# Streaming v twice: 256 instead of 128 columns in each product of the attention sums

## The chip, the cores and the metric

The kernel runs on one core of a Trainium2 chip. The metric is the device time of one execution in microseconds, lower is better. A core has TensorE (PE; its weight loads are listed as PEld), VectorE (DVE), ScalarE (ACT), GpSimd (POOL), SyncE (SP) and 16 DMA engines.

## The reference

A sampled attention is followed by a feed-forward block that only 128 tokens of each batch pass through. Sizes are B = 8 batches, H = 8 heads, S = 576 positions, head size 64, 32 memory slots, D = 512, F = 1024, capacity 128.

```python
a = exp(phi - max(phi)) ; a = a / (sum(a) + 1e-9)     # over the 32 slots
k_m = einsum('bhsm,bhsd->bhmd', a, k)
v_m = einsum('bhsm,bhsd->bhmd', a, v)                 # the sums that the change touches
attn = softmax(q @ k_m.T / sqrt(64))
x = (attn @ v_m)                                      # heads joined: (B, S, 512)
scores = einsum('bsd,d->bs', x, w_gate)
for b in range(B):
    top_idx = argpartition(-scores[b], 128)[:128]
    ye = maximum(x[b, top_idx] @ w1, 0) @ w2
    out[b, top_idx] = x + sigmoid(scores) * ye        # other rows: out = x
```

## The kernel before

The softmax of phi is written out in some thirty VectorE and ScalarE instructions per batch (two chains take the batches in turn). `keys` turns its result over on TensorE (line 559), writes it to DRAM in two parts (`aparts`) and forms k_m (line 598). `split_v` writes v to DRAM in two parts as well (`vparts`).

The sums v_m are formed in `values`. The positions of a batch are cut into 48 chunks of T = 12 steps. Four batches are live at a time, one in each band of 32 partitions, and one accumulator bank of PSUM (`accs`) belongs to each. Batches 0 to 3 begin 6 chunks apart, batches 4 to 7 follow 48 chunks later in the same bands, which makes 114 chunks. For a chunk, `a_loader` (SyncE, line 640) fetches the softmax rows into `a_flat`, `widener` (lines 688 and 690, on VectorE or ScalarE) spreads them into `a_rows` (two buffers), and `v_loader` (POOL's queue, line 664) fetches `v_rows` (three buffers). A buffer is filled again when the products of the chunk that read it are through. Then each step issues one product for each live batch (line 709): the stationary operand is 32 rows by 128 columns of `a_rows`, the moving operand 32 rows by 128 values of `v_rows`, both in fp32r, and the result is added in 128 columns of the batch's bank.

When a batch's sums are complete, line 725 turns them over, `centre`, `scores` and `attend` (lines 770 to 933) do the attention, `rank` (lines 944 to 993) chooses the 128 tokens, and `forward` (lines 1055 to 1104) gathers them and runs two layers in fp32 (lines 1075 and 1093).

All of these are generators. `in_order_of_time` picks the next one by times that `Plan` keeps while the program is written: it books a duration for every instruction and, for TensorE, an amount of activity, from which `speed` decides which of the two clocks it books next. For products in fp32r the duration is `share`, set by `values` from the number of live batches, and the activity goes with the columns of `rhs`. While it books the lower clock, `forward` is given preference. So each engine's order is fixed when the program is written; on the chip each engine runs its own queue in that order.

Of the kernel before, what the change touches and what calls it, by code (L numbers as in the profile page):

```python
# [21 lines left out]
P = 128  # L22
# [164 lines left out]
def kernel(  # L187
# [15 lines left out]
    nc = Machine(plan, tc.nc)  # L203
# [6 lines left out]
    NG = phiT.shape[1]  # L210
    H = NG * NPR
    Dh = D // H
# [3 lines left out]
    SET = 4  # L216
# [5 lines left out]
    def first(b):  # L222
        return b // SET * STEP + b % SET * LAG
# [18 lines left out]
    accs = [psum.tile([P, 512], F32, name=f"acc{i}") for i in range(SET)]  # L242
# [28 lines left out]
    def take(n=1):  # L271
        while len(banks) < n:
            yield lambda: len(banks) >= n
        got = [first_free() for _ in range(n)]
        return got if n > 1 else got[0]
# [84 lines left out]
    def copy(dst, src):  # L360
        nc.scalar.activation(dst, src, AF.Copy)
        return plan.end
# [252 lines left out]
    def live(ch):  # L615
        return [b for b in range(B) if first(b) <= ch < first(b) + n_pieces]
# [82 lines left out]
    def values():  # L699
        for ch in range(COLS // T):  # L700
            while ch >= len(widened) or ch >= len(v_loaded):
                yield lambda: ch < len(widened) and ch < len(v_loaded)
            yield max(widened[ch], v_loaded[ch])
            vr, ar = v_rows[ch % NV], a_rows[ch % NB]
            plan.share = 256.0 / len(live(ch))
            for s in range(T):
                for b in live(ch):
                    p = slice(b % SET * 32, b % SET * 32 + 32)
                    nc.tensor.matmul(out=accs[b % SET][:, :P].rearrange("p (g d) -> p g d", d=Dh),  # L709
                                     lhsT=ar[p, s].rearrange("p j m -> p (j m)"), rhs=vr[p, :, s],  # L710
                                     start=(ch == first(b) and s == 0),
                                     stop=(ch == first(b) + n_pieces - 1 and s == T - 1))
                if s % 3 == 2 and s < T - 1:
                    yield plan.free["pe"]
            used_up.append(plan.end)
            b = live(ch)[0]
            if ch == first(b) + n_pieces - 1:
                yield
                turned = work.tile([P, P], F32, name="turned", tag="vz", bufs=1)
                copy(turned, accs[b % SET][:, :P])  # L720
                if b >= B - SET:
                    banks.append([plan.end, accs[b % SET]])
                yield
                bk = yield from take()
                nc.tensor.transpose(out=bk([P, P]), in_=turned, identity=ident)
                yield
                copy(v_m[b], bk([P, P]))
                bk.give()
                summed[b] = plan.end
# [382 lines left out]
    def load_weights():  # L1112
# [26 lines left out]
        (0.5 * 1e3, keys()), (0.0 * 1e3, split_v()),  # L1139
        (0.0, phi_loader()), (0.0, k_loader()), (0.0, q_loader()), (0.0, a_loader()), (0.0, v_loader()), (0.0, widener()),  # L1140
        (0.0 * 1e3, values()), (0.0 * 1e3, attentions(0)), (0.0 * 1e3, attentions(1)),
        (None and None * 1e3, forward(B * nt)), (0.0, load_weights())])

# [48 lines left out]
```

## Time and profile before

| what | value |
|---|---|
| median of three runs | 799.24 us |
| profiled execution, its own time | 798.46 us |
| its span, first to last instruction | 796.8 us |
| PE busy | 567.5 us, 71% |
| DVE busy | 587.7 us, 74% |
| ACT busy | 364.8 us, 46% |
| POOL busy | 235.6 us, 30% |
| products of the sums (line 709) | 4608, 265.7 us busy |

The span lies inside the execution's own time; 1.7 us lie around it. Busy time counts a time in which at least one instruction of the engine runs; products overlap on TensorE, so a mean duration is longer than the spacing of products. The clock column (PEclk) is the share of 2.4 GHz that was granted.

### The profile page before, as it was taken

To read this page: it belongs to the slowest core of one execution; us is meant where nothing else is said; L and a number is where in the kernel's file an instruction comes from. 1 tells how busy PE (TensorE), PEld (TensorE's weight loads), DVE (VectorE), ACT (ScalarE), POOL (GpSimd) and SP (SyncE) were. 2 spreads that over 40 slices of the span, in tenths; PEclk is the share of its full clock that TensorE was granted. 3 is DMA by queue.
4 is the path that set the end of the run, shared out by engine and by line. 5 is a ranking of instruction groups with operands and counts; after the bars stand their busy time and mean duration, and the time that the engine had idled before them with its cause. 6 is when DMAs were issued, how large, how long until landed. Compare 5 with 4: busy or idle time off the path is not lost. (4 is left out here: it accounts for less than half of the span.)

```text
span 796.8 us, 17830 instructions
## 1 busy us (share of the span) xinstructions
PE 567.5 (71%) x6898; PEld 462.8 (58%) x6898; DVE 587.7 (74%) x1043; ACT 364.8 (46%) x649; POOL 235.6 (30%) x419
## 2 busy tenths in 40 slices
PE   0002046145282499688997999999998999999994
PEld 0001045045271488677876778868877768766672
DVE  5999999999999999689628565658524387687700
ACT  3344462456355476464625436355634246434310
POOL 5022343423322233324314122315344142211200
PEclk9999999999999999999998558669899679899998
DMA  6046755879746577889666454548665434311110
GB/s 176 0 158 206 249 184 198 297 205 274 235 156 200 153 239 247 259 240 278 192 211 209 140 163 135 186 127 269 200 204 173 141 111 128 121 66 47 60 40 18
DMA packets 70348, 137.32 MB, mean 172 GB/s; under 512 B 14064, under 2 KB 46832, under 8 KB 70256
## 3 DMA queue, kind: packets, MB, share of 16 engines
q0 software_dynamic: 21824, 79.72, 30.4%
q1 hardware_dynamic: 48432, 56.39, 24.5%
q8 instruction: 56, 0.92, 0.5%
q14 instruction: 36, 0.29, 0.1%
HBM read 96.21 MB, written 39.85 MB: 171 GB/s over the span
## 5 line engine op out<-in xcount | busy, mean ns | idle before, releaser
L709 PE MATMUL acc<-v_rows,a_rows 32*128 32x128 f32 x4608 | 265.7, 360 | 60.1 <-ACT a_rows L690 32.4
L709 PEld LDWEIGHTS acc<-v_rows,a_rows 32*128 32x128 f32 x4608 | 245.2, 270 | 105.9 <-issue 43.4
L664 POOL DMA_DIRECT2D v_rows<-vparts x228 | 130.6, 580 | 284.5 <-PE acc L709 283.3
L690 ACT ACTIVATE a_rows<-a_flat,block_of 128x384 fp32r<-128x384 f32 x264 | 143.1, 604 | 137.1 <-PE acc L709 61.5
L688 DVE TENSOR_SCALAR a_rows<-a_flat,block_of 128x384 fp32r<-128x384 f32 x192 | 71.8, 419 | 80.1 <-PE acc L709 37.9
L559 PE MATMUL bank<-ident,ph 128*96 128x128 f32 x96 | 26.6, 432 | 77.3 <-DVE ph L464 77.3
L559 PEld LDWEIGHTS bank<-ident,ph 128*96 128x96 f32 x96 | 16.5, 198 | 81.4 <-issue 63.2
L598 PE MATMUL bank<-kb,aS 96*32 96x64 f32 x768 | 25.5, 308 | 51.6 <-DMA kb<-in_k 51.6
L1075 PE MATMUL bank<-xeT,w 128*128 128x128 f32 x416 | 57.0, 294 | 1.4 <-ACT xeT L1059 1.4
L1075 PEld LDWEIGHTS bank<-xeT,w 128*128 128x128 f32 x416 | 52.7, 205 | 4.1 <-ACT xeT L1059 1.8
L1093 PE MATMUL bank<-w,hT 128*128 128x512 f32 x96 | 54.8, 703 | 0.0
L533 POOL DMA_DIRECT2D vparts<-vlo x32 | 18.2, 569 | 121.5 <-DVE vlo L529 115.0
L598 PEld LDWEIGHTS bank<-kb,aS 96*32 96x32 f32 x768 | 19.9, 164 | 56.0 <-issue 26.1
L874 PE MATMUL bank<-vbd,eT 128*128 128x256 f32 x120 | 47.9, 546 | 0.0
L965 DVE SCALAR_TENSOR_TENSOR marks<-row,tg,wide 128x576 bf16<-128x576 f32 x40 | 32.7, 818 | 10.7 <-ACT row L949 9.0
L918 POOL DMA_DIRECT2D out<-xj x24 | 16.4, 682 | 64.7 <-DVE xj L914 55.4
L874 PEld LDWEIGHTS bank<-vbd,eT 128*128 128x128 f32 x120 | 29.7, 269 | 7.4 <-issue 1.7
L961 ACT ACTIVATE marks<-row,tg 128x576 bf16<-128x576 f32 x40 | 31.0, 775 | 1.8
L1093 PEld LDWEIGHTS bank<-w,hT 128*128 128x128 f32 x96 | 19.7, 222 | 17.7 <-issue 15.5
L461 DVE SCALAR_TENSOR_TENSOR ph<-rh,sm,ph 128x576 f32<-128x576 f16 x32 | 25.9, 810 | 4.3 <-ACT rh L450 4.3
L905 DVE TENSOR_TENSOR xj<-bank,rd 128x512 f32<-128x512 f32 x30 | 20.2, 684 | 10.8 <-PE bank L874 9.3
L924 DVE TENSOR_TENSOR prod<-xj,wg 128x512 f32<-128x512 f32 x40 | 27.4, 684 | 0.4
(163 smaller groups left out, 940.9 us busy)
## 6 DMA issues: line engine op xcount, KB each, us to landing
v_rows<-vparts POOLq DMA_DIRECT2D x156, 192.0 KB, 4.2
a_flat<-aparts SPq DMA_DIRECT2D x312, 48.0 KB
vb<-in_v SPq DMA_DIRECT2D x32, 288.0 KB
kb<-in_k SPq DMA_DIRECT2D x32, 288.0 KB
vparts<-vlo POOLq DMA_DIRECT2D x32, 288.0 KB, 2.9
vparts<-vb POOLq DMA_DIRECT2D x32, 288.0 KB, 4.0
qb<-in_qT SPq DMA_DIRECT2D x16, 576.0 KB
out<-xj POOLq DMA_DIRECT2D x16, 512.0 KB, 3.2
```

The costliest lines, as they stand in the source:

```text
L559: nc.tensor.transpose(out=bk([PT, 3, P])[:, c], in_=a[:, c0 + c], identity=ident)
L598: nc.tensor.matmul(out=km[j * M:(j + 1) * M], lhsT=aS[g][:, j, c], rhs=kb[:, j, c % (NC // 2)], start=(c == 0), stop=(c == NC - 1))
L664: nc.gpsimd.dma_start(out=v_rows[ch % NV].bitcast(F32)[32 * r0 + g:32 * r1:2, g] .rearrange("p s d -> p (s d)"), in_=src[:, ch * T * Dh:(c ...
L688: nc.vector.tensor_scalar_mul(ar[:, :, j], src, block_of[:, j:j + 1])
L690: nc.scalar.activation(ar[:, :, j], src, AF.Copy, scale=block_of[:, j:j + 1])
L709: nc.tensor.matmul(out=accs[b % SET][:, :P].rearrange("p (g d) -> p g d", d=Dh), lhsT=ar[p, s].rearrange("p j m -> p (j m)"), rhs=vr[p, :, s],
L874: nc.tensor.matmul(out=o([P, D])[:, g * 4 * Dh:(g + 1) * 4 * Dh], lhsT=eT[:, g, c * P:(c + 1) * P], rhs=vbd[b % 2][:, g].rearrange("p j d ...
L924: nc.vector.tensor_mul(prod, x[:, c], wg)
L961: nc.scalar.activation(sign, row, AF.Sign, bias=g, scale=-1.0, accum_out=less[:, c:c + 1])
L965: nc.vector.scalar_tensor_tensor(out=cmp, in0=row, scalar=g, in1=wide[:, off:off + S], op0=ALU.is_equal, op1=ALU.mult, accum_out=equal[:, ...
L1075: nc.tensor.matmul(out=bk([P, 4, P])[:, f, :n], lhsT=w1_sb[d][:, (f0 + f) * P:(f0 + f + 1) * P], rhs=xeT[:, d, :n], start=(d == 0), stop=( ...
L1093: nc.tensor.matmul(out=ps[:n], lhsT=hT[:, f, :n], rhs=w2_sb[f], start=(f == 0), stop=(f == KF - 1))
```

## The change

Each product of the sums takes the 128 values of v twice, by a repeat with stride 0 in the access pattern of the moving operand, and adds its result in 256 columns of the accumulator bank. The second 128 columns hold the same sums as the first; lines 720 and after read the first 128 alone. The bank has 512 columns. The number of products, their stationary operands and all transfers stay the same. `Plan.matmul` counts the cells of `rhs`, so the activity it books for these products doubles; the duration that it books stays.

```diff
             for s in range(T):
                 for b in live(ch):
                     p = slice(b % SET * 32, b % SET * 32 + 32)
-                    nc.tensor.matmul(out=accs[b % SET][:, :P].rearrange("p (g d) -> p g d", d=Dh),
-                                     lhsT=ar[p, s].rearrange("p j m -> p (j m)"), rhs=vr[p, :, s],
+                    nc.tensor.matmul(out=accs[b % SET][:, :2 * P].rearrange("p (r g d) -> p r g d", g=NG, d=Dh),
+                                     lhsT=ar[p, s].rearrange("p j m -> p (j m)"),
+                                     rhs=vr[p, :, s].unsqueeze(1).to_broadcast([32, 2, NG, Dh]),
                                      start=(ch == first(b) and s == 0),
                                      stop=(ch == first(b) + n_pieces - 1 and s == T - 1))
                 if s % 3 == 2 and s < T - 1:
```

## Rows read from the trace of the kernel before

**Rows 1.** The page's slices: 40 equal parts of the span, busy tenths.

```profile
PE   0002046145282499688997999999998999999994
DVE  5999999999999999689628565658524387687700
```

**Rows 2.** Windows of all engines: busy us (instructions), granted clock, DMA share, GB/s.

```profile
core 0: us, PE busy (x) PEld busy (x) DVE busy (x) ACT busy (x) POOL busy (x), PEclk, DMA share, GB/s
263.70:289.70 26.00, 19.56 (x372) 18.28 (x376) 25.93 (x35) 15.21 (x19) 10.13 (x16) 1.00 0.67 208
289.70:385.00 95.30, 79.67 (x1390) 72.32 (x1386) 81.01 (x124) 56.56 (x94) 32.39 (x56) 1.00 0.82 246
385.00:417.70 32.70, 32.35 (x363) 25.92 (x359) 12.78 (x35) 12.55 (x30) 8.34 (x15) 1.00 0.68 206
417.70:701.10 283.40, 273.03 (x3422) 218.49 (x3421) 170.11 (x428) 132.20 (x291) 89.68 (x156) 0.78 0.52 162
500.00:600.00 100.00, 99.32 (x1554) 79.50 (x1553) 54.76 (x136) 47.97 (x99) 37.20 (x64) 0.83 0.63 196
```

**Rows 3.** Line 709 in 296 to 306, then 424 to 431 us: duration ns min/median/max.

```profile
L709 PE MATMUL acc<-v_rows,a_rows x164: 410/410/471, 295.8 to 305.9; 32*128 32x128 f32 x164
...
L709 PE MATMUL acc<-v_rows,a_rows x156: 267/270/323, 424.9 to 430.6; 32*128 32x128 f32 x156
```

**Rows 4.** Timeline of PE in four places: start us, us, what, count.

```profile
295.76 5.96 PE L709 MATMUL acc<-v_rows,a_rows 32*128 32x128 f32 x108
...
424.90 2.57 PE L709 MATMUL acc<-v_rows,a_rows 32*128 32x128 f32 x84
428.42 2.41 PE L709 MATMUL acc<-v_rows,a_rows 32*128 32x128 f32 x72 [0.95 <-ACT a_rows L690]
...
464.88 4.75 PE L709 MATMUL acc<-v_rows,a_rows 32*128 32x128 f32 x84
```

**Rows 5.** Timeline at 110 us, one batch live: loads and products in turn.

```profile
110.23 0.54 PEld L709 LDWEIGHTS acc<-v_rows,a_rows 32*128 32x128 f32 x2
...
110.34 0.41 PE L709 MATMUL acc<-v_rows,a_rows 32*128 32x128 f32 x1
...
110.44 0.33 PEld L709 LDWEIGHTS acc<-v_rows,a_rows 32*128 32x128 f32 x1
...
110.55 0.62 PE L709 MATMUL acc<-v_rows,a_rows 32*128 32x128 f32 x2
```

**Rows 6.** Windows of line 709 alone, the last three at the lower clock.

```profile
0.00:263.70 263.70, 50.71 (x432) 47.45 (x432) 1.00 0.62 194
263.70:289.70 26.00, 17.32 (x300) 16.38 (x304) 1.00 0.67 208
289.70:385.00 95.30, 66.16 (x1148) 62.49 (x1144) 1.00 0.82 246
385.00:417.70 32.70, 14.58 (x228) 12.89 (x228) 1.00 0.68 206
417.70:701.10 283.40, 116.08 (x2502) 105.25 (x2502) 0.78 0.52 162
431.40:482.60 51.20, 19.57 (x312) 17.51 (x312) 0.50 0.49 156
503.10:523.60 20.50, 9.87 (x180) 9.30 (x172) 0.50 0.63 191
622.50:643.00 20.50, 7.83 (x99) 7.27 (x99) 0.50 0.44 135
```

**Rows 7.** What PE waited for, 289.7 to 417.7: us, times, longest.

```profile
PE bank L598 <- DMA kb<-in_k: 6.5, 4, 2.4
PE acc L709 <- DMA v_rows<-vparts: 6.3, 3, 4.9
```

**Rows 8.** Who waited for the sums, 417.7 to 701: us, times, longest.

```profile
POOL v_rows L664 <- PE acc L709: 156.5, 47, 13.3
ACT a_rows L690 <- PE acc L709: 55.0, 23, 13.7
...
DVE a_rows L688 <- PE acc L709: 32.1, 25, 4.4
```

## The prediction

> **What bounds the kernel now.** I read the page's slices first [rows 1]. For the first 300 us VectorE is 9 in nearly every slice while TensorE is mostly under 6, so the softmax on VectorE sets the pace; from about 400 us to the end TensorE is 9 in nearly every slice and VectorE mostly under 7. So extra TensorE time should be cheap early and paid in full late. The windows of all engines put numbers to it [rows 2]: TensorE has 6.4 us idle of 26.0 up to 289.7, 15.6 of 95.3 up to 385, 0.35 of 32.7 up to 417.7, and 10.4 of 283.4 from there until the last sums. In the stretch up to 385 the DMA share is 0.82: transfers are close behind as a second pace.
>
> The second thing to read is TensorE's clock. The windows give a mean granted clock of 0.78 from 417.7 to 701.1 [rows 2]. With levels of 1.2 and 2.4 GHz, (1 - 0.78) x 2 = 44% of 283.4 us, so 125 us, ran at 1.2 GHz. Before 417.7 the clock column says 1.00, but I do not believe it: one product of the sums lasts 410 ns at the median at 296 to 306 us and 270 ns at 424 to 431 us [rows 3]. The work is the same, so the first stretch ran at 1.2 GHz as well. The timeline agrees: 84 products took 4.75 us at 464.88, inside a stretch with granted clock 0.50, and 2.57 us at 424.90 [rows 4, 6].
>
> **What one step costs now.** With four batches live, a step s of a chunk is four products, one in each 32-row band, that run side by side. In the half clock 108 products are 27 steps, 26 spacings and the last product's 0.41 us: (5.96 - 0.41)/26 = 213 ns. In the full clock 84 products are 21 steps: (2.57 - 0.27)/20 = 115 ns [rows 4]. That is about 256 and 276 array cycles for 128 columns. Where the other half goes shows where a single batch is live [rows 5]: a weight load starts at 110.23, its product at 110.34, the next load at 110.44, the next product at 110.55. Load and stream take turns, 105 to 110 ns each, that is 128 columns each at 1.2 GHz: the next load into the band begins when the stream is through.
>
> **The change part by part.** It adds no instruction, transfer or wait. It doubles the columns of 4608 products. By the alternation above the load stays 128 columns and the stream becomes 256: a step gains 107 ns at 1.2 GHz (213 to 320) and 53 ns at 2.4 GHz (115 to 168). That the second pass re-reads the same SBUF values and writes unread PSUM columns I cost at nothing, since the rate per column comes from the same streams. There are 114 chunks x 12 = 1368 steps. I count them by stage from the products [rows 6]: 432 products up to 263.7 are chunks 0 to 17, 216 steps; then at four products a step 300, 1148 and 228 products are 75, 287 and 57 steps; the other 733 come after 417.7.
>
> Stage one, up to 263.7: 216 x 107 = 23 us more work. TensorE runs sums for 50.7 us of 263.7 there [rows 6], and VectorE covers it [rows 1]. I take 0; if the cover fails, 23 us. What could break the cover is the widening of a_rows on VectorE and ScalarE, which waits for the chunk two before: if it comes later, the softmax instructions queued behind it on these engines come later too.
>
> Stage two, 263.7 to 417.7: 419 steps x 107 ns = 45 us more work against 22.4 us of idle time [rows 2]. After 289.7 most of TensorE's own waits end with a transfer: 6.5 us for kb and 6.3 us for v_rows [rows 7]. A later TensorE finds most of these landed, though some were issued only when an earlier product had freed the buffer and move along with it. If all the idle time fills, 22 us are left over. It is less if part of this stage rises to 2.4 GHz: a step is then 168 instead of 213 ns, 45 ns below today's, and the bound is 419 x 45 = 19 us below nothing. The upper bound is all 45 us. I take half of the 22, +11 us, since the stretch also has full-array transposes beside the sums but is mostly sums and narrow products.
>
> Stage three, 417.7 to the last sums: TensorE is full, so 733 x 53 = 39 us are paid in full even at 2.4 GHz. Three of the half-clock stretches hold 312, 180 and 99 products [rows 6], about 78 + 45 + 40 = 163 steps in 92 of the 125 us; I take 190 steps for all. If the clock stays as it is, these pay another 190 x 53 = 10 us: +49 us is the upper bound. The other end is the clock. Streaming now fills two thirds of a step (256 of 384 columns), where it filled half (128 of 256). If that gives back every half-clock stretch, 125 us become 62: 39 - 62 = -23 us. In the three stretches the sums are 38%, 48% and 38% of the time [rows 6]; the rest is products that the change leaves alone. So I take half of the 125 us as regained: -31 us, and 95 steps still at 1.2 GHz, +5 us. Together 39 + 5 - 31 = +13 us.
>
> On the clock the rows say that a busy engine alone doesn't hold it: from 500 to 600 us TensorE is busy for 99.32 us of 100 at a mean of 0.83 [rows 2], and sums alone at 464.88 stay in the half clock [rows 4]. The Trainium skill (TensorE: Matmul & The Clock Gate, Why this matters for your kernels) asks for a TensorE kept busy continuously to reach the full clock; the trace has it busy and not at full clock, so the measurement decides, and what the extra columns do is open in size.
>
> The planner that orders the program books the columns of each product as activity, so it books the sums twice as high, and keeps their time as it was. Its picture of the clock, and so the place of the feed-forward products among the sums, will differ. On a full engine an order is worth little: after 417.7 TensorE has 10.4 us of idle time in all [rows 2]. I take 0, with 10 us either way. The longer hold on a chunk's buffers delays three waits that already stand there: POOL for v_rows 156.5 us in 47 waits, ScalarE 55.0 us in 23 and VectorE 32.1 us in 25 for a_rows [rows 8]. Queued behind them are POOL's stores of the attention output and gathers for the feed-forward, and the softmax's or attention's instructions. While TensorE is the bound I cost this at nothing; with TensorE starved it would be paid.
>
> After 701 us there are almost no sums; nothing changes. Sum: 798.46 us of the profiled execution (span 796.8) + 0 + 11 + 13 = 822 us; the median of the runs, 799.24, is 0.1% off, so I do not correct.
>
> **The rivals.** First, the covers hold: stage two hides wholly in idle time and transfers, and stage three regains rather more clock: 0 + 4 gives about 803. For it speaks the DMA share of 0.82, against it the 45 us of work against 22 us idle.
>
> Second, the other side, the clock comes back: with two thirds of a step streaming the sums hold 2.4 GHz wherever they run after 417.7. With stage two hidden that is -23 us, 776 us. With x of the 125 us regained stage three costs 49 - 0.58 x, so it decides from x = 85 us on, and from 103 us if stage two still costs 11. For it: the long fall at 431 us comes right after a run of sums alone at full clock [rows 4]; against it: much of the half-clock time is other work.
>
> Third, the load hides behind the longer stream: a step stays at 213 and 115 ns, 256 columns, nothing is added, and the clock regained is a gain of 0 to 31 us (half the 125 us regained): 767 to 798, in the middle 783. Against it the load in rows 5 starts only when the stream before it ends. The Trainium skill (TensorE: Matmul & The Clock Gate, Part 2, on the loading of weights) says that a load may be pulled ahead of running products when it goes to another row group or to the background weight buffer; with the second the load would vanish under 256 columns. The trace of the sums shows no such pull within one band.
>
> Fourth, the clock doesn't move: 22 + 49 = +71 us, 870 us. For it: sums alone never left the half clock in the rows. Against it: the sums are mixed with full-array products in most of stage three.
>
> **How the numbers follow.** Forecast 822 with chance 0.48, covers hold 0.22, clock back 0.11, load hidden 0.08, clock unmoved 0.11. The likeliest alone spans 808 to 850: stage two from 0 to 22 us and stage three from +9 to +30 us. The 8-in-10 range takes in the covers and the hidden load and leaves out most of the two extremes, clock back below and clock unmoved above: 780 to 855. A measurement of this kernel tells some 2% from no change, so faster is below 783 and slower above 815. Slower: most of the forecast, 0.42, and the fourth, 0.11, give 0.53. Faster: the clock back and a part of the hidden load, 0.15. Within 2%: 0.32.
>
> **What would show it.** In the changed kernel, right: steps of four sums spaced some 320 and 165 ns, a load starting a full 256 columns after its product; TensorE full from earlier, about 290 us; the first attention (lines 725 and 770) later than now; mean granted clock between 417 us and the last sums above 0.85; the tail after the last sums unchanged. Wrong: a spacing still at 213 or 115 ns (hidden load), a spacing above these (a slower rate for the repeated stream), the median duration of a sum before 417 us near 2.4 GHz's, or a clock as low as today's. The number fails most easily in the half taken of the clock: 25 us regained more or less move it by 12.

## The result and the profile after

The changed kernel takes 762.08 us at the median of four runs; the kernel before takes 798.76 us over the runs beside it. The ratio is 0.957, with a 95% interval of 0.951 to 0.964. Runs in a slower state, such as one of the kernel before at 817.35 us, are left out of the ratios. The forecast was 822 us, slower by 3%, with a range of 780 to 855. The direction was wrong.

The page's slices, to be laid beside [rows 1]:

```profile
PE   0002029027364256756599889998999999999994
DVE  4999999999999999979856787778224877589400
PEclk9999999999995568978888899999899996899998
```

The picture is the same up to the middle: VectorE paces the first half, TensorE the second. New is the clock row. The recorded clock now starts to move at slice 12, at about 230 us, where it falls to 5 (slices counted from 0), and from slice 18 on it is 8 or 9 in all slices but one. The 9 before that is no full clock: as in the kernel before, products last 410 ns there (below). The windows of all engines, to be laid beside [rows 2]; the fourth runs to the last sum, which comes at 653.4 us instead of 701.7:

```profile
263.70:289.70 26.00, 15.45 (x360) 13.99 (x360) 25.93 (x37) 15.19 (x19) 9.88 (x16) 0.73 0.64 198
289.70:385.00 95.30, 63.08 (x1415) 55.05 (x1419) 81.81 (x121) 61.94 (x105) 33.32 (x57) 0.80 0.83 252
385.00:417.70 32.70, 30.50 (x545) 24.04 (x543) 20.59 (x53) 15.57 (x37) 11.63 (x21) 0.86 0.81 245
417.70:653.50 235.80, 224.91 (x3147) 179.79 (x3139) 154.08 (x391) 122.71 (x272) 84.59 (x148) 0.91 0.59 182
653.50:759.60 106.10, 93.46 (x567) 69.38 (x565) 51.05 (x117) 27.45 (x66) 13.71 (x18) 0.97 0.17 57
```

From 289.7 to 385 us TensorE is busy for less time than before, 63.1 instead of 79.7 us, though its products are twice as wide. From 417.7 us to the last sum the mean granted clock is 0.91 instead of 0.78, and the stretch is 47.6 us shorter (235.8 instead of 283.4). The tail behind it is 10 us longer (106.1 instead of 95.7): more feed-forward is left over when the sums end.

Line 709 of the changed kernel, products first at 110 us and then at 303 us (duration ns min/median/max, first and last start), beside [rows 3]:

```profile
L709 PE MATMUL acc<-v_rows,a_rows x9: 410/410/548, 109.7 to 111.5; 32*128 32x256 f32 x9
...
L709 PE MATMUL acc<-v_rows,a_rows x96: 272/278/382, 302.7 to 305.5; 32*128 32x256 f32 x96
```

A product of 256 columns lasts 410 ns at 1.2 GHz and 278 ns at 2.4 GHz. One of 128 columns lasted 410 and 270. The doubled stream does not show in the duration. Nor does it in the spacing: 96 products are 24 steps, whose starts lie between 302.7 and 305.5 us, (305.5 - 302.7)/23 = 122 ns a step, against 115 ns before [rows 4]. Over all runs of sums alone at 2.4 GHz in the two traces the median step is 120 and 112 ns. The timeline of loads and products with one batch live, beside [rows 5] (the first row of each pair is the product, the second the next load):

```profile
110.04 0.41 PE L709 MATMUL acc<-v_rows,a_rows 32*128 32x256 f32 x1
110.04 0.33 PEld L709 LDWEIGHTS acc<-v_rows,a_rows 32*128 32x128 f32 x1
...
110.25 0.41 PE L709 MATMUL acc<-v_rows,a_rows 32*128 32x256 f32 x1
110.25 0.33 PEld L709 LDWEIGHTS acc<-v_rows,a_rows 32*128 32x128 f32 x1
```

Product and next load now start together, 0.21 us apart from pair to pair: the same 213 ns a step as before. The load that I had seen start only "when the stream is through" starts with the product.

### The profile page after: what moved, and what is told of

The parts are those of the page before. It is cut to its first block, busy times and chain, and to the rows that moved or that the text cites. A ratio compares the mean times of both kernels' runs of the same rounds, so it can differ in the third digit from the quotient of the medians.

```text
span 759.6 us, 17829 instructions
## 1 busy us (share of the span) xinstructions
PE 506.1 (67%) x6898; PEld 408.1 (54%) x6898; DVE 584.8 (77%) x1035; ACT 367.7 (48%) x657; POOL 235.1 (31%) x419
## 4 chain that ended last, share of the span: by engine, by line
PE 38%; DVE 31%; DMA 10%; SPq 7%; issue 6%; ACT 6%; POOL 1%; DVEq 0%; ACTq 0%; POOLq 0%
PE acc L709 12%; DMA a_flat<-aparts 8%; SPq L640 7%; PE bank L1076 5%; PE bank L875 4%; PE bank L1094 4%; ACT a_rows L690 3%; DVE a_rows L688 2%; DVE vlo L529 2%; PE acc L1076 2%; PE acc L1094 2%; DVE num L404 2%; DVE num L402 2%; DVE vlo L527 1%; DVE ph L461 1%
## 5 line engine op out<-in xcount | busy, mean ns | idle before, releaser
L709 PE MATMUL acc<-v_rows,a_rows 32*128 32x256 f32 x4608 | 239.6, 319 | 79.6 <-DVE a_rows L688 27.4
L709 PEld LDWEIGHTS acc<-v_rows,a_rows 32*128 32x128 f32 x4608 | 210.4, 217 | 118.2 <-ACT a_rows L690 53.7
L690 ACT ACTIVATE a_rows<-a_flat,block_of 128x384 fp32r<-128x384 f32 x272 | 147.3, 605 | 115.3 <-PE acc L709 49.0
L559 PE MATMUL bank<-ident,ph 128*96 128x128 f32 x96 | 22.4, 377 | 80.1 <-DVE ph L464 80.1
L533 POOL DMA_DIRECT2D vparts<-vlo x32 | 18.2, 568 | 121.3 <-DVE vlo L529 117.3
L1076 PE MATMUL bank<-xeT,w 128*128 128x128 f32 x384 | 52.1, 292 | 1.2 <-ACT xeT L1060 1.2
L1076 PEld LDWEIGHTS bank<-xeT,w 128*128 128x128 f32 x384 | 48.2, 203 | 4.4 <-ACT xeT L1060 2.1
L875 PE MATMUL bank<-vbd,eT 128*128 128x256 f32 x128 | 40.5, 455 | 0.0
L1094 PE MATMUL bank<-w,hT 128*128 128x512 f32 x80 | 38.1, 607 | 0.0
L928 DVE TENSOR_REDUCE four<-prod 128x128 f32<-128x512 f32 x40 | 27.2, 680 | 0.6
L915 DVE TENSOR_TENSOR xj<-xj,mean 128x1024 f32<-128x1024 f32 (+1 forms) x24 | 25.0, 1042 | 0.3
```

The source lines that it names most:

```text
L559: nc.tensor.transpose(out=bk([PT, 3, P])[:, c], in_=a[:, c0 + c], identity=ident)
L690: nc.scalar.activation(ar[:, :, j], src, AF.Copy, scale=block_of[:, j:j + 1])
L709: nc.tensor.matmul(out=accs[b % SET][:, :2 * P].rearrange("p (r g d) -> p r g d", g=NG, d=Dh), lhsT=ar[p, s].rearrange("p j m -> p (j m)") ...
L875: nc.tensor.matmul(out=o([P, D])[:, g * 4 * Dh:(g + 1) * 4 * Dh], lhsT=eT[:, g, c * P:(c + 1) * P], rhs=vbd[b % 2][:, g].rearrange("p j d ...
L1076: nc.tensor.matmul(out=bk([P, 4, P])[:, f, :n], lhsT=w1_sb[d][:, (f0 + f) * P:(f0 + f + 1) * P], rhs=xeT[:, d, :n], start=(d == 0), stop=( ...
L1094: nc.tensor.matmul(out=ps[:n], lhsT=hT[:, f, :n], rhs=w2_sb[f], start=(f == 0), stop=(f == KF - 1))
```

## The experiments

Ratios are to the runs of the kernel before on the same chip, with the 95% interval in brackets.

**Order or columns?** The change does two things: it doubles the columns, and through the planner it moves work on every engine. Two kernels did one each.

```diff
 # e1: 128 columns as before, in Plan.matmul
-            cycles, used = self.share, N * K / P
+            cycles, used = self.share, 2 * N * K / P
```

> 128 columns as before; only the planner books the sums' activity twice, so the order on every engine is that of the changed kernel. If the new order brought the gain: about 762 us (ratio 0.955). If the columns brought it through TensorE's clock: about 799 us, within 1.5% of before, with half-clock stretches of 100 us or more after 417 us, since the sums stream no more than before. In between: both take part.

```diff
 # e2: 256 columns as in the change, in Plan.matmul
-            cycles, used = self.share, N * K / P
+            cycles, used = self.share, P * K / P
```

> 256 columns; the planner books the sums as before, so the order on every engine is that of the kernel before. If the columns brought the gain: 755 to 775 us, with the half-clock time after 417 us down from about 123 us to 30 to 60 us and steps at 213 and 120 ns. If the order did: about 799 us.

The order alone took 806.29 us, ratio 1.013 (1.007 to 1.019): a little slower. The columns alone took 762.50 us, ratio 0.962 (0.955 to 0.969): the whole gain. Windows of all engines from 417.7 to 640 us, a stretch that holds sums in every kernel: first the kernel before, then e1, then e2 (clock, DMA share and GB/s are the last three numbers):

```profile
417.70:640.00 222.30, 213.33 (x2957) 172.23 (x2959) 124.35 (x311) 100.96 (x219) 71.89 (x125) 0.76 0.56 176
```

```profile
417.70:640.00 222.30, 214.70 (x3008) 177.58 (x3010) 128.44 (x326) 102.79 (x224) 72.91 (x128) 0.75 0.56 178
```

```profile
417.70:640.00 222.30, 214.73 (x3093) 171.98 (x3090) 148.15 (x377) 116.28 (x256) 80.42 (x141) 0.95 0.60 188
```

TensorE is as full in all three, 213 to 215 us of 222.3; the clock differs, 0.76 and 0.75 against 0.95.

**What a step costs.** Two kernels gave every chunk its own width. These and the following kernels, up to the one with 384 columns, book the activity of the sums as e2 does, so their order is that of the kernel before. The extra columns are the neighbours of v's values in `v_rows` (padded at its end) and are written beside the sums.

```diff
+    SIZES = [512, 128, 160, 192, 224, 240]    # p2: [512, 256, 248, 252, 320, 384]
...
+                    w = SIZES[ch % len(SIZES)] // 2
-                    nc.tensor.matmul(out=accs[b % SET][:, :P].rearrange("p (g d) -> p g d", d=Dh),
-                                     ... rhs=vr[p, :, s],
+                    nc.tensor.matmul(out=accs[b % SET].rearrange("p (g d) -> p g d", g=NG)[:, :, :w],
+                                     ... rhs=vr.rearrange("p g s d -> p g (s d)")[p, :, s * Dh:s * Dh + w],
```

> The width of the sums' products goes by chunk: 512, 128, 160, 192, 224, 240 columns in turn (extra columns are neighbours of v's values, written beside the sums and unread); the order is that of before. It is made for the spacing of products at 1.2 GHz where one batch is live, 110 to 180 us. Theory A, load and stream take turns below 256 columns: (128 + N)/1.2, so 213, 240, 267, 293, 307 ns for 128 to 240, and 427 ns (N alone) for 512. Theory B, a stream of under 256 columns runs at half rate: N/0.6, so 213, 267, 320, 373, 400 ns, and 427 ns for 512. Theory C, a step has a floor of 256 columns: 213 ns for all five, and 427 ns for 512.

> As the run before with widths of 512, 256, 248, 252, 320, 384 columns by chunk. At 1.2 GHz, 512, 256, 320 and 384 columns take N/1.2 in every theory: 427, 213, 267, 320 ns, with the load pulled under the stream. 248 and 252 tell where the behaviour changes: theory A (128 + N)/1.2 gives 313 and 317 ns, theory B 413 and 420 ns, theory C 213 ns for both.

The products of one chunk each, one batch live, at 1.2 GHz; the spacing is the difference of first and last start over the count less one. First p1, then p2:

```profile
L712 PE MATMUL acc<-v_rows,a_rows x11: 623/623/623, 111.2 to 115.5; 32*128 32x512 f32 x11
...
L712 PE MATMUL acc<-v_rows,a_rows x12: 410/410/465, 118.5 to 120.9; 32*128 32x160 f32 x12
...
L712 PE MATMUL acc<-v_rows,a_rows x12: 410/410/437, 121.1 to 123.5; 32*128 32x192 f32 x12
...
L712 PE MATMUL acc<-v_rows,a_rows x12: 410/410/423, 126.8 to 129.2; 32*128 32x240 f32 x12
```

```profile
L712 PE MATMUL acc<-v_rows,a_rows x12: 410/410/410, 116.3 to 118.7; 32*128 32x256 f32 x12
...
L712 PE MATMUL acc<-v_rows,a_rows x12: 410/410/543, 118.9 to 121.4; 32*128 32x248 f32 x12
...
L712 PE MATMUL acc<-v_rows,a_rows x12: 463/463/628, 124.7 to 127.8; 32*128 32x320 f32 x12
...
L712 PE MATMUL acc<-v_rows,a_rows x12: 517/517/517, 128.0 to 131.5; 32*128 32x384 f32 x12
```

From 160 to 256 columns the twelve starts take 2.4 to 2.5 us, so 218 to 227 ns a step with the first wait in it, whatever the width. Above it the width counts: 320 columns 282 ns with the first wait, 384 columns 318 ns, 512 columns 430 ns, as N/1.2 says (267, 320, 427). Theory C, a floor of 256 columns, holds; the theory of my prediction (A) would have 240 columns at 307 ns and is refuted, and so is the half-rate stream (B) with 400. The whole times, 832.03 and 823.48 us, mix six widths and are only the price of the wide chunks.

What makes the floor? A third kernel also narrowed the stationary operand. It leaves out some of the sums, and its spacing alone is read.

```diff
+    SIZES = [(128, 128), (64, 128), (32, 128), (64, 256), (96, 128), (128, 64)]
...
+                    m, n = (P, 2 * P) if ch == first(b) and s == 0 else SIZES[ch % len(SIZES)]
-                    nc.tensor.matmul(out=accs[b % SET][:, :P] ..., lhsT=ar[p, s] ..., rhs=vr[p, :, s],
+                    nc.tensor.matmul(out=o, lhsT=ar[p, s, :m // M] ..., rhs=x,    # m by n of them
```

> Width of the stationary operand M and columns N go by chunk: (128,128), (64,128), (32,128), (64,256), (96,128), (128,64); the first product of each batch is (128,256). With M under 128 the sums of some heads are left out, with N = 64 those of half the head groups. Read at 1.2 GHz with one batch live, 110 to 180 us. Theory L, the weight load of a product takes two column times for each of its M columns and runs beside the stream: the spacing is the larger of 2 M and N columns, so 213, 107, 107, 213, 160, 213 ns. Theory F, every such product has a floor of 256 columns, whatever is loaded: 213 ns for all six.

Its chunks at 110 to 130 us, the operand's partitions by stationary columns first:

```profile
L716 PE MATMUL acc<-v_rows,a_rows x12: 281/303/303, 115.0 to 116.2; 32*32 32x128 f32 x12
...
L716 PE MATMUL acc<-v_rows,a_rows x13: 303/303/410, 112.0 to 113.4; 32*64 32x128 f32 x12, 32*128 32x128 f32 x1
...
L716 PE MATMUL acc<-v_rows,a_rows x9: 410/410/441, 116.7 to 118.4; 32*64 32x256 f32 x9
...
L716 PE MATMUL acc<-v_rows,a_rows x9: 357/357/417, 124.8 to 126.1; 32*96 32x128 f32 x9
...
L716 PE MATMUL acc<-v_rows,a_rows x5: 396/396/415, 127.2 to 128.1; 32*128 32x64 f32 x5
```

Again the spacing is the difference of first and last start over the count less one. With 32 stationary columns and 128 streamed it is 1.2/11 = 109 ns, with 64 it is 1.4/12 = 117 ns, one wider product of the chunk before included. With 64 and 256: 1.7/8 = 213 ns. With 96 and 128: 1.3/8 = 163 ns. With 128 and only 64 streamed: 0.9/4 = 225 ns, no less than with 128. The first and last starts are rounded to 0.1 us; single starts in the trace lie 107, 107, 213, 160 and 213 ns apart. Every one is the larger of 2 M and N column times, a column time being the 1/1.2 ns in which one column streams at 1.2 GHz. So theory L holds: the weight load of these fp32r products takes two column times for each stationary column, 256 for 128, it runs beside the stream, and it sets the step. The durations go the same way, though the profile models the ends of products. A product lasts 410 ns where the step is 213, 357 at 160 and 303 at 107: some 197 ns more than the step each time, whether the load sets it or, as with 320, 384 and 512 columns (463, 517 and 623 ns), the stream; only the 64 streamed columns fall short, with 396.

This also fits [rows 5]. In p1 a load starts 0.13, 0.16, 0.19 and 0.20 us before its own product with 160, 192, 224 and 240 columns, which is the time of one stream of that width. So it seems that a product is recorded once the one before it has streamed, and not when its own stream begins. In the kernel before, loads ran back to back, 0.21 us apart from 110.23 to 110.44; each product was recorded as soon as the one before had streamed its 107 ns, and then it waited for its weights. This is a reading of the records; no run shows the beginning of a stream itself.

**Is it the clock?** If a step costs the same from 128 to 256 columns, a width between must gain part of the time through the clock alone. Two kernels with p1's buffers and one width each:

```diff
+    SIZES = [192]        # and [256] as its control
```

> 192 columns in every product of the sums (the extra 64 are neighbours of v's values, unread), order of before. The step's spacing stays 213 and 112 ns as at 128 and 256 columns. Theory clock (the gain comes from more columns streamed in the same time, which holds the clock up): between the two kernels, 770 to 792 us, with some 50 to 110 us at 1.2 GHz between 417 us and the last sums. Theory spacing (256 columns unlock something in the sums that 192 do not): about 797 us.

> The control of the run before: same buffers and neighbours, 256 columns. 758 to 768 us, as the changed kernel; if the layout of the buffers costs something, it shows here.

192 columns took 782.02 us, ratio 0.980 (0.962 to 0.997); the control took 762.71 us, 0.961 (0.949 to 0.974), as the changed kernel. The four runs with 192 columns, 774 to 788 us, lie clear of the control's, 759 to 764 us, and just touch those of the kernel before, 785 to 815 us. The windows of e4_n192 and of e4_n256:

```profile
417.70:640.00 222.30, 209.42 (x3063) 165.63 (x3053) 137.94 (x349) 109.94 (x242) 79.85 (x139) 0.87 0.60 186
```

```profile
417.70:640.00 222.30, 212.22 (x3072) 169.94 (x3068) 146.13 (x371) 113.84 (x252) 78.67 (x137) 0.95 0.60 185
```

At nearly the same cost of a step (213 ns at 1.2 GHz for all three, and medians of 112, 112 and 120 ns at 2.4 GHz), granted clocks of 0.76, 0.87 and 0.95 go with 798, 782 and 762 us for 128, 192 and 256 columns. Up to its last sum the run with 192 columns has a mean clock of 0.84 over 269.8 us, so 86 us at 1.2 GHz, inside the 50 to 110 us expected; the control has 0.93 over 245.5 us, so 34 us, and the kernel before 125 us.

**Where is it earned?** The wide products in the first 48 chunks alone, then in the others alone:

```diff
+                    r = 2 if ch < 48 else 1      # late: 2 if ch >= 48 or (ch == first(b) and s == 0)
+                    ... out=accs[b % SET][:, :r * P] ..., rhs=vr[p, :, s].unsqueeze(1).to_broadcast([32, r, NG, Dh]),
```

> 256 columns for chunks 0 to 47 alone (until about 385 us), 128 after; order of before. If, as the comparison of the traces says, VectorE and the transfers pace the kernel up to there, the gain is small: 788 to 797 us. If the early clock brought the gain: 765 to 775 us.

> 256 columns for chunks 48 to 113 alone (and for the first product of each batch), 128 before; order of before. Most of the gain comes from here: 762 to 772 us, and what is missing to the changed kernel is what the early run gains. If the early clock brought the gain: 788 to 800 us.

Early alone took 806.13 us, 1.018 (1.002 to 1.034), no gain and above the 788 to 797 us expected; late alone 761.08 us, 0.959 (0.945 to 0.973), the whole gain. Windows of e5_early, before 385 us and after 417.7, and of e6_late:

```profile
263.70:385.00 121.30, 83.49 (x1794) 73.69 (x1794) 110.05 (x167) 74.39 (x121) 42.49 (x72) 0.74 0.82 245
417.70:640.00 222.30, 213.35 (x2790) 172.22 (x2779) 118.22 (x299) 97.23 (x213) 67.50 (x118) 0.73 0.54 170
```

```profile
417.70:640.00 222.30, 211.46 (x3099) 168.27 (x3091) 145.84 (x372) 115.82 (x255) 81.03 (x142) 0.95 0.61 189
```

In the early run TensorE has the full clock for part of the time up to 385 us and is busy for 83.5 of 121.3 us, where it was busy for 19.56 + 79.67 = 99.2 [rows 2]: the time saved is idle time, for VectorE and the transfers set the pace there. That the run is, if anything, a little slower than the kernel before goes with the clock behind it: 0.74 over the 291.9 us from 417.7 us to its last sum, so 152 us at 1.2 GHz against 125 us. Why the clock falls more there is open.

**Is still more better?** Three times the values, 384 columns:

```diff
-                                     rhs=vr[p, :, s].unsqueeze(1).to_broadcast([32, 2, NG, Dh]),
+                                     rhs=vr[p, :, s].unsqueeze(1).to_broadcast([32, 3, NG, Dh]),
```

> Each product streams v's values three times, 384 columns; order of before. The stream is now longer than the load: steps of 320 and 175 ns against 213 and 120. The clock is held at least as well as with 256. After 417 us some 730 steps cost 55 ns more, +40 us, against at most 20 us that the clock can still give: 782 to 802 us. Under 770 us would say that the clock is worth more than the steps.

It took 791.81 us, ratio 1.004 (0.996 to 1.011). Its window:

```profile
417.70:640.00 222.30, 220.06 (x2975) 177.03 (x2975) 133.20 (x338) 105.78 (x228) 76.85 (x132) 0.98 0.56 177
```

The clock is higher yet, 0.98, and the time of the kernel before is back, as expected: now the stream is the longer part of a step (384 columns: 320 ns at 1.2 GHz in p2, a median of 174 ns at 2.4 GHz in this trace) and is paid in full.

**A better order?** Two kernels changed the planner only, with the change's 256 columns. The first took the full clock for granted from 400 us on and so gave the feed-forward no preference there; the second gave it always.

```diff
 # v1, in Plan.speed and in_order_of_time
-        return 1 / 2.4 if self.warm.get(k, False) else 1 / 1.2
+        return 1 / 2.4 if t > 4e5 or self.warm.get(k, False) else 1 / 1.2
...
-                x[0] - 12 * 1e3 if not plan.warm.get(plan.at) else max(x[0], free))
+                x[0] - 12 * 1e3 if not plan.warm.get(plan.at) and free < 4e5 else max(x[0], free))
 # v2, in in_order_of_time of the change
-                x[0] - 12 * 1e3 if not plan.warm.get(plan.at) else max(x[0], free))
+                x[0] - 12 * 1e3)
```

Both book the activity of 256 columns, as the change does.

> The changed kernel (256 columns) with a planner that books the full clock from 400 us of its own time on, as the trace now shows it, and gives the feed-forward no preference from there. The order changes alone. TensorE has little idle time there, so 750 to 768 us; it beats the changed kernel if the planner's picture of the clock still misplaces work.

> The changed kernel (256 columns) with the feed-forward always given the preference that it now has only while the planner books the lower clock: the opposite of the run that gave it none from 400 us on. If feed-forward products early are what keeps the clock up and the end short, 745 to 762 us; if the preference delays the sums, 765 to 785 us.

Both missed. v1 took 782.07 us, 0.983 (0.972 to 0.994), 20 us more than the change; v2 took 873.68 us, 1.103 (1.091 to 1.115). For v2 a part of the cause shows in the window and in what TensorE waited for there (us, times, longest):

```profile
417.70:640.00 222.30, 180.51 (x2418) 142.58 (x2418) 101.33 (x251) 82.13 (x178) 58.55 (x100) 0.85 0.44 144
```

```profile
PE bank L1056 <- DMA xe<-out,idx: 19.1, 4, 6.6
PE acc L709 <- ACT a_rows L690: 12.1, 9, 2.4
```

TensorE is idle for 42 of 222 us. In four of the waits, 19.1 us, feed-forward products stand in its queue and wait for their gathered rows, and what stands behind them waits too. The clock is lower as well: from 417.7 us to the last sum, at 767.4 us, it is 0.80, so 140 us ran at 1.2 GHz where the change has 42. In v1 it is 0.87 over the 247.0 us to the last sum, so 64 us, and the tail behind the last sum is 118 us long instead of 106; how much each is worth the runs do not separate. No version beat the change by more than the runs scatter.

## Why the prediction was wrong

**The step of the sum that failed** is the cost of a step: "the load stays 128 columns and the stream becomes 256: a step gains 107 ns at 1.2 GHz (213 to 320) and 53 ns at 2.4 GHz (115 to 168)". Measured: 0 ns at 1.2 GHz and 7 ns at 2.4 GHz (115 to 122). With these the same working gives nothing for stage two and 5 - 31 = -26 us for stage three, so 772 us, a gain; the other 10 us go with the clock's term, which was put too low (stage three below). The alternation of starts was read rightly and interpreted wrongly: the load, not load plus stream, fills the 256 column times, and there was room for 128 more columns beside it. This is the third rival, which I gave a chance of 0.08: a load and a stream that overlap, though the other way round than I put it. With 128 columns the stream hides beside the longer load. The Trainium skill (TensorE: Matmul & The Clock Gate, Part 2, on the loading of weights) states that a load is pulled ahead of running products when it targets the background weight buffer. The runs agree that a load overlaps a product within one band: load and product start together at 110.04 us, and a step of 384 columns takes 320 ns, the time of its stream alone. My sentence that the trace shows no such pull was wrong.

**Stage one** was 0 and stayed 0: 432 products are done by 263.7 us in both. **Stage two** was put at +11 us; it ends ahead instead. Windows of line 709 alone in the changed kernel, beside [rows 6]:

```profile
0.00:263.70 263.70, 50.19 (x432) 45.16 (x432) 0.94 0.62 194
263.70:289.70 26.00, 13.54 (x288) 12.34 (x288) 0.73 0.64 198
289.70:385.00 95.30, 52.53 (x1196) 46.67 (x1200) 0.80 0.83 252
385.00:417.70 32.70, 15.30 (x358) 12.61 (x356) 0.86 0.81 245
```

By 385 us 1916 products are done against 1880, by 417.7 us 2274 against 2108. Most of the lead comes after 385 us, where TensorE was full [rows 2] and had the half clock and now has 0.86. The first attention (line 770, 771 in the changed kernel) begins at 392 us instead of 400 us; I had expected it later.

**Stage three** was put at 39 + 5 - 31 = +13 us. In place of the 39 and the 5 stand 733 x 7 ns = 5 us. The clock's term was right in mechanism and too small: I took half of 125 us as regained, -31 us. Now (1 - 0.91) x 2 x 235.8 = 42 us up to the last sum run at 1.2 GHz, so 83 us were regained, worth up to 41. In [rows 4] a run of sums alone stands just before the long fall at 431 us; in the changed kernel 96 sums in a row at 303 us keep the full clock, 278 ns a product at the median. Counted from 385 us to the end, the half-clock time went from 33 + 125 + 8 to 9 + 42 + 6 us (the 33 us up to 417.7 because products last 411 ns there at the median, the others from the granted clock). Half of the 109 us is 54 us, less 5 for the steps 49; the span from there shrank from 411.8 to 374.6 us, by 37. So the clock is more than enough for the gain. That some 12 us of it were not earned I take for time in which TensorE's rate was not what was waited for, such as chains of single dependent products; the runs do not separate that. The runs with 192 and 256 columns, and the wide products late alone, show the clock's part without this sum.

**The planner's order** at 0 with 10 us either way: e1 shows +1.3%, 10 us, with 128 columns, and the change against e2 shows none with 256. But "on a full engine an order is worth little" is too strong: v1 is 20 us slower than the change and v2 112 us. The order moves the clock too, of which the 10.4 us of idle time that the prediction went by say nothing.

**The buffer waits**, costed at nothing, became shorter. What waited for the sums in the changed kernel, 417.7 to 653.5 us, beside [rows 8]:

```profile
POOL v_rows L664 <- PE acc L709: 105.6, 43, 10.5
ACT a_rows L690 <- PE acc L709: 34.9, 21, 7.1
DVE a_rows L688 <- PE acc L709: 27.0, 19, 4.1
```

**The rivals.** The third had the right mechanism in part, at 767 to 798 us; it missed 762 because it regained at most half of the clock. The first, covers that hold, and the second, the clock comes back, gave 803 and 776 us with the wrong price of a step in them. The fourth is refuted by the clock of 0.91.

## What to carry to other kernels

When loads and products alternate in a trace, find out which of them sets the spacing before adding to the other: a spacing of starts that does not change with the width of the products, or a run with a narrower stationary operand, tells it. Where the weight load is the longer part, as with these fp32r products, moving columns cost next to nothing up to its length (0 ns a step at 1.2 GHz, 7 ns at 2.4 GHz). On an engine that is full but runs at half clock even useless ones can pay, by holding the clock. Past that length the same columns cost their full time: 384 lost what 256 had won.

## What the runs showed of the hardware that was not expected

- The weight load of an fp32r product takes two column times for each stationary column: steps of 213, 160 and 107 ns at 1.2 GHz for 128, 96 and 64 or fewer stationary columns with 128 streamed.
- A product's record seems to hold the wait for its weights: with 128 stationary columns 128 and 256 streamed columns both show 410 ns, and 128 streamed columns with 64 stationary ones show 303 ns. The profile models the ends, so this is a reading.
- More columns streamed in the same step held TensorE's clock higher: 0.76, 0.87 and 0.95 from 417.7 to 640 us with 128, 192 and 256 columns, with TensorE busy for 209 to 213 us of 222.3 in each.
- The clock column of a profile can read 1.00 where products run at the half clock: before 417.7 us in the kernel before, 410 against 270 ns.
